# Row stores over all DMA engines, and k loaded in 1 KB pieces for the first two batches

## The chip, the core and the metric

The kernel runs on one core of one Trainium2 chip. The metric is the device time of one execution in microseconds; the runs of one kernel lie mostly within 0.3% of their median, so differences of 2 us out of 930 need several runs. The core has TensorE (PE, its weight loads as PEld), VectorE (DVE), ScalarE (ACT), GpSimd (POOL), and the sync engine (SP), which here issues almost all DMAs. All runs below were in the fast state.

## The reference

```python
kv  = np.einsum('bhsd,bhse->bhde', k, v)          # 8 batches, 8 heads, 576 rows, 64 wide
out = np.einsum('bhsd,bhde->bhse', q, kv)
rms = np.sqrt(np.mean(out * out, axis=-1, keepdims=True) + 1e-06)
x   = (out / rms * g_norm)                        # -> (4608, 512)
h   = x @ w_in                                    # 512 -> 2048
g   = np.maximum(h, 0.0) + np.log1p(np.exp(-np.abs(h)))
y   = g @ w_out                                   # 2048 -> 512
```

## The kernel before

All work is entered as tasks with an engine, a planned duration in ns and a priority (`pos`). At build time a small scheduler in the kernel orders the tasks of each engine; at run time each engine goes through its list in that order. 40 tuned numbers (`P0`) give priorities to the first weights (conversion and fetch), the first tiles and batches, and the later weights. While TensorE has nothing planned before the first matmul of the MLP (the two products with w_in and w_out), filler matmuls (`warm`) are put in, which are meant to keep its clock up.

The sums kv. Of each batch there are four loads of k and of v, each with the first 512 rows of two heads, four neighbouring rows to a partition (4 x 64 numbers, 1 KB), and one tail with the last 64 rows of all heads:

```python
x = new(s, [P, H, D])
src = src[b, p::NP, :MAIN].rearrange("h (s i) d -> s h i d", i=4)
if s is ks:
    for h in range(2):
        nc.sync.dma_start(out=x[:, h::2], in_=src[:, h])       # 256 B pieces
else:
    nc.sync.dma_start(out=x.rearrange("s (h i) d -> s h i d", h=2), in_=src)   # 1 KB pieces
# ... (cut)
for i in range(4):
    # l: two heads of k side by side, r: the same two heads of v
    nc.tensor.matmul(kv[:, i if tail else p], lhsT=l, rhs=r, ...)   # 128 x 128, half of it unused
last = add("PE", 820, run, lds + [last], pos + 0.5 * p, ...)
```

x leaves for DRAM in blocks of three tiles (TB = 3, 384 rows). From tile 12 on it is transposed in 32 x 32 blocks by VectorE and written three tiles together, which permutes the rows within a block; the result of a tile therefore leaves in up to four pieces of 32 rows:

```python
if ph == LAST and t >= BY_PE:
    n, i = divmod(t, TB)
    def store():
        m = 0
        while m < P // BL:                        # BL = 32
            a, u = divmod(P // BL * i + m, TB)
            k = min(TB - u, P // BL - m)
            nc.sync.dma_start(
                out=out[n * NT:(n + 1) * NT].rearrange("(t s) f -> t s f", t=TB)[u:u + k, a * BL:(a + 1) * BL],
                in_=ot.tile[m * BL:(m + k) * BL])
            m += k
    part[ph, t] = None, add("SP", 800, store, [a], pos, [], [ot], 750)
    return
dst = out[t * P:(t + 1) * P] if ph == LAST else ...            # whole rows of earlier tiles
```

The head of the program, which the experiments come to:

```python
for e in range(2):
    nc.scalar.dma_start(out=g_col[e * D:(e + 1) * D], in_=...)
nc.scalar.mul(g_down, g_col, DOWN_G)
nc.scalar.preload_act_table_set("softplus")
scratch = kv_diag[0][:, 0]
make_identity(nc, scratch)
```

## Time and profile before

| | before |
|---|---|
| time, median of 3 | 934.63 us |
| span of the profiled run | 932.7 us |
| TensorE idle, 0 to 55 us | 11.4 us |
| filler matmuls, 0 to 55 us | 43, 15.9 us |
| TensorE idle, 55 to 916.3 us | 0.04 us |
| from the last matmul to the end | 16.4 us |

TensorE's time can be read as three parts: a start in which it is idle, filled or busy by turns; a long middle in which it is always busy; and an end in which only data leave. The start and the end are what this change can move. The lines that carry this stand in the prediction.

### The profile page before, as it was taken

To read this page: it belongs to the slowest core of one execution; us is meant where nothing else is said; L and a number is where in the kernel's file an instruction comes from. 1 tells how busy PE (TensorE), PEld (TensorE's weight loads), DVE (VectorE), ACT (ScalarE), POOL (GpSimd) and SP (SyncE) were. 2 spreads that over 40 slices of the span, in tenths; PEclk is the share of its full clock that TensorE was granted. 3 is DMA by queue.
4 is the path that set the end of the run, shared out by engine and by line. 5 is a ranking of instruction groups with operands and counts; after the bars stand their busy time and mean duration, and the time that the engine had idled before them with its cause. 6 is when DMAs were issued, how large, how long until landed. Compare 5 with 4: busy or idle time off the path is not lost.

```text
span 932.7 us, 13257 instructions
## 1 busy us (share of the span) xinstructions
PE 904.9 (97%) x4821; PEld 818.5 (88%) x4821; DVE 627.3 (67%) x1055; ACT 414.5 (44%) x799; POOL 80.4 (9%) x78
## 2 busy tenths in 40 slices
PE   7899999999999999999999999999999999999992
PEld 5689899989999999999999999989999998999992
DVE  6777788776458887788757878887434455655531
ACT  4766555444433656464424455555322323333320
POOL 0323421221113100000000000000000000000000
PEclk8999999999999999999999999999999999999997
DMA  8999998498782554346334445551231233444321
GB/s 213 225 225 222 248 212 205 102 212 151 171 143 90 147 147 136 112 145 206 102 102 128 148 157 169 189 182 39 85 102 56 81 102 102 106 119 127 109 75 42
DMA packets 231377, 131.43 MB, mean 141 GB/s; under 512 B 130448, under 2 KB 205200, under 8 KB 231312
## 3 DMA queue, kind: packets, MB, share of 16 engines
q1 hardware_dynamic: 231152, 130.58, 53.3%
q8 instruction: 38, 0.62, 0.3%
q14 instruction: 27, 0.22, 0.1%
q10 hardware_dynamic: 160, 0.00, 0.0%
HBM read 91.75 MB, written 38.80 MB: 140 GB/s over the span
## 4 chain that ended last, share of the span: by engine, by line
PE 93%; SPq 2%; DVE 1%; DMA 1%; POOL 1%; ACT 1%; issue 0%; ACTq 0%
PE s L665 43%; PE h L658 43%; PE o L523 3%; PE o L506 3%; SPq L568 1%; DMA g_col<-in_g_norm_dram 1%; PE tp L540 0%; POOL r L532 0%; DMA m<-in_v_dram 0%; DMA qa<-in_q_dram 0%; DVE m L312 0%; PE tp L578 0%; DVE r L528 0%; DVE xv L440 0%; DVE m L316 0%
## 5 line engine op out<-in xcount | busy, mean ns | idle before, releaser
L658 PE MATMUL h<-xv,w 128*128 128x384 f32 x2304 | 434.6, 337 | 0.0
L665 PE MATMUL s<-w,gv 128*128 128x512 f32 x1728 | 434.3, 395 | 0.0
L658 PEld LDWEIGHTS h<-xv,w 128*128 128x128 f32 x2304 | 406.2, 188 | 14.8 <-issue 0.2
L665 PEld LDWEIGHTS s<-w,gv 128*128 128x128 f32 x1728 | 319.5, 188 | 59.1 <-issue 0.5
L678 ACT ACTIVATE g<-h 128x384 f32<-128x384 f32 x192 | 94.3, 491 | 398.4 <-PE h L658 394.4
L669 DVE TENSOR_TENSOR gv<-g,gv 128x384 fp32r<-128x384 f32 x192 | 106.6, 555 | 175.9 <-ACT gv L680 175.0
L680 ACT ACTIVATE gv<-g 128x384 fp32r<-128x384 f32 x192 | 100.9, 525 | 23.3 <-PE s L665 16.6
L673 DVE SCALAR_TENSOR_TENSOR gv<-gv 128x384 fp32r<-128x384 f32 x192 | 107.0, 557 | 6.0
L440 DVE SCALAR_TENSOR_TENSOR xv<-m,g_col,xv 128x512 fp32r<-128x512 f32 x102 | 75.8, 743 | 1.1 <-ACT xv L437 1.1
L444 DVE SCALAR_TENSOR_TENSOR xv<-xv 128x512 fp32r<-128x512 f32 x108 | 74.5, 690 | 2.6
L437 ACT ACTIVATE xv<-m,g_down 128x512 fp32r<-128x512 f32 x102 | 69.7, 710 | 2.5 <-DMA m<-x 2.4
L532 POOL TENSOR_TENSOR r<-r,half 128x8 f32<-128x8 f32 x36 | 65.8, 1826 | 3.0
L506 PEld LDWEIGHTS o<-m,m 128*128 128x128 f32 x256 | 34.2, 200 | 8.7 <-issue 7.3
L506 PE MATMUL o<-m,m 128*128 128x128 f32 x256 | 35.4, 285 | 6.4 <-DMA m<-in_v_dram 6.4
L705 DVE SCALAR_TENSOR_TENSOR m<-s,scale,m 128x512 f32<-128x512 f32 x24 | 17.9, 747 | 29.7 <-PE s L665 29.7
L523 PE MATMUL o<-kv_diag,m 128*128 128x128 f32 (+1 forms) x296 | 36.9, 275 | 0.0
L523 PEld LDWEIGHTS o<-kv_diag,m 128*128 128x128 f32 (+1 forms) x296 | 35.0, 179 | 1.8 <-issue 1.0
L531 POOL TENSOR_SCALAR r<-r 128x8 f32<-128x8 f32 x36 | 13.9, 386 | 244.9 <-DVE r L528 244.8
L535 DVE TENSOR_TENSOR x<-o,r 128x512 f32<-128x512 f32 x33 | 22.7, 688 | 17.6 <-POOL r L532 17.6
L528 DVE TENSOR_REDUCE r<-x 128x8 f32<-128x512 f32 x36 | 24.5, 681 | 13.3 <-ACT x L591 13.2
L705 DVE SCALAR_TENSOR_TENSOR m<-s,m 128x512 f32<-128x512 f32 x36 | 23.3, 684 | 10.2 <-PE s L665 10.1
L286 ACT ACTIVATE sq<-raw 128x512 bf16<-128x512 bf16 x32 | 21.3, 665 | 16.4 <-DMA raw<-in_moe_w_in_dram 10.2
(67 smaller groups left out, 445.6 us busy)
## 6 DMA issues: line engine op xcount, KB each, us to landing
m<-x SPq DMA_DIRECT2D x102, 256.0 KB
part<-m SPq DMA_DIRECT2D x72, 256.0 KB
m<-part SPq DMA_DIRECT2D x72, 256.0 KB
raw<-in_moe_w_in_dram SPq DMA_DIRECT2D x16, 512.0 KB
m<-in_k_dram SPq DMA_DIRECT2D x64, 128.0 KB
m<-in_v_dram SPq DMA_DIRECT2D x32, 256.0 KB
raw<-in_moe_w_out_dram SPq DMA_DIRECT2D x16, 512.0 KB
qa<-in_q_dram SPq DMA_DIRECT2D x24, 288.0 KB
```

What stands on the lines that cost most here:

```text
L437: nc.scalar.activation(cols(0, F32R), x.tile, func=AF.Identity, scale=g_down)
L440: nc.vector.scalar_tensor_tensor(out=cols(1, F32R), in0=x.tile, scalar=g_col, in1=cols(0), op0=ALU.mult, op1=ALU.subtract)
L444: nc.vector.scalar_tensor_tensor(out=cols(2, F32R), in0=cols(1), scalar=-RADIX, in1=cols(0), op0=ALU.mult, op1=ALU.add)
L506: nc.tensor.matmul(kv[:, i if tail else p], lhsT=l, rhs=r, start=(p == 0 and i == 0), stop=tail, skip_group_check=True)
L523: nc.tensor.matmul(y[r0:r0 + n, p::NP], lhsT=qT.tile[:, p, r0:r0 + n], rhs=kv_diag[b % 2][:, p].rearrange("r (h d) -> r h d", d=D), start= ...
L532: nc.gpsimd.tensor_tensor(out=r.tile, in0=r.tile, in1=half, op=ALU.pow)
L658: nc.tensor.matmul(hp, lhsT=w_in.tile[:, i, kd * P:(kd + 1) * P], rhs=xv.tile[:, i, kd], start=(m == 0), stop=(m == 3 * KD - 1))
L665: nc.tensor.matmul(mine[i].tile, lhsT=gv.tile[:, m, i * P:(i + 1) * P], rhs=w_out.tile[:, m], start=(c == cs[0] and m == 0), stop=(c == cs ...
L669: nc.vector.tensor_tensor(out=gv.tile[:, 1], in0=g.tile, in1=gv.tile.bitcast(F32)[:, 0], op=ALU.subtract)
L673: nc.vector.scalar_tensor_tensor(out=gv.tile[:, 2], in0=f32[:, 1], scalar=-RADIX, in1=f32[:, 0], op0=ALU.mult, op1=ALU.add)
L678: a = add("ACT", 490, lambda: nc.scalar.activation(new(g, [P, NT]), h.tile, func=AF.Softplus, scale=1.0 + E), [a], s, [g], [h])
L680: a = add("ACT", 530, lambda: nc.scalar.activation(new(gv, [P, 3, NT], F32R)[:, 0], g.tile, func=AF.Copy, scale=DOWN), [a], s, [gv])
```

## The change

The intent is to let the last results leave over all DMA engines, and to get the first k sooner. In the diff the 40 priorities are cut to their first three.

```diff
-    P0 = [-93.0, -6.2, -50.8, ...]      # 40 numbers
+    P0 = [-71.0, -4.7, -70.3, ...]
@@ kv_of
+        wide_rows = b < 2
-                if s is ks:
+                if s is ks and not wide_rows:
@@ run
+                    if wide_rows and not tail:
+                        for e in range(2):
+                            l, r = (x.tile.rearrange("s (h i) d -> s h i d", h=2)[:, e, i] for x in (ks, vs))
+                            nc.tensor.matmul(kv[e * D:(e + 1) * D, p, e], lhsT=l, rhs=r, ...)   # 64 x 64
+                        continue
-            last = add("PE", 820, run, ...
+            last = add("PE", 1640 if wide_rows and not tail else 820, run, ...
@@ rows: x of the last block is written tile by tile
+        g = TB if n < n_blocks - 1 else 1
+        i0, i = i - i % g, i % g
@@ leave
-        if ph == LAST and t >= BY_PE:
+        if ph == LAST and BY_PE <= t < n_tiles - TB:
-                (the while loop over k tiles)
+                for m in range(P // BL):
+                    a, u = divmod(P // BL * i + m, TB)
+                    row = n * NT + u * P + a * BL
+                    nc.sync.dma_start(out=out[row:row + BL], in_=ot.tile[m * BL:(m + 1) * BL])
```

The sums go a head at a time with this layout: the four rows of a head now lie side by side, so the same row of two heads no longer does. Not printed above are the planned durations that follow: 500 ns for a wide k load instead of 900, and 1600 ns for the four stores of a tile instead of 800.

More of the change, by code (lines that the diff above doesn't have):

```diff
@@ L184 @@
     LAST = PHASES[-1]
-    P0 = [-93.0, -6.2, -50.8, -8.7, -11.6, -1.5, -14.9, 2.7, -53.5, -34.8, -51.7, -14.7, -24.2, 1.3,
-          -0.2, -4.2, 2.5, -13.0, 8.5, 9.5, 5.5, 23.5, -2.0, 2.5, 2.5, 7.0, 5.0, 14.5, 9.0, 44.5, 49.5,
-          68.5, 52.5, 72.0, 95.5, 100.5, 114.5, 111.0, 116.5, 8.5]
+    P0 = [-71.0, -4.7, -70.3, -8.7, -15.1, -0.5, -23.9, 2.7, -65.0, -28.3, -35.2, -10.7, -25.2, 1.3,
+          -0.2, -2.7, 0.5, -17.5, 13.0, 9.5, 5.5, 6.5, -2.0, 2.5, 2.5, 28.0, 15.0, 14.5, 8.5, 44.5,
+          49.5, 68.5, 52.5, 72.0, 94.5, 99.5, 115.5, 110.5, 114.5, 8.5]
     CONVERT, FETCH, EARLY, LATER = P0[:8], P0[8:16], P0[16:27], P0[27:]
@@ L495, in kv_of @@
                        620 if tail else size, behind=int(pos - 2) - 3)
-                   for src, s, ns, size in ((k, ks, 900, 1300), (v, vs, 500, 850))]
+                   for src, s, ns, size in ((k, ks, *((500, 850) if wide_rows and not tail else (900, 1300))), (v, vs, 500, 850))]
             def run(ks=ks, vs=vs, p=p, tail=tail, n=n):
@@ L500, in run @@
                 for i in range(4):
+                    if wide_rows and not tail:
+                        for e in range(2):
+                            l, r = (x.tile.rearrange("s (h i) d -> s h i d", h=2)[:, e, i] for x in (ks, vs))
+                            nc.tensor.matmul(kv[e * D:(e + 1) * D, p, e], lhsT=l, rhs=r, start=(p == 0 and i == 0),
+                                             stop=False, skip_group_check=True)
+                        continue
                     if tail:
@@ L507, in run @@
                                      skip_group_check=True)
-            last = add("PE", 820, run, lds + [last], pos + 0.5 * p,
+            last = add("PE", 1640 if wide_rows and not tail else 820, run, lds + [last], pos + 0.5 * p,
                        [bank] if p == 0 else [], [ks, vs])
@@ L613, in turn_blocks @@
             if i == 0:
-                new(xb, [P, d_model // BL, TB, BL])
+                new(xb, [P, d_model // BL, g, BL])
             nc.vector.transpose(out=xb.tile[:, :, i], in_=x.tile.rearrange("p h d -> p (h d)").rearrange(
@@ L618, in store @@
         def store(a):
-            nc.sync.dma_start(out=xd[n][:, a * TB * BL:(a + 1) * TB * BL].rearrange("(b i) m -> i b m", i=BL),
+            nc.sync.dma_start(out=xd[n][:, i0 * P + a * g * BL:i0 * P + (a + 1) * g * BL].rearrange("(b i) m -> i b m", i=BL),
                               in_=xb.tile[a * BL:(a + 1) * BL].rearrange("i b t j -> i b (t j)"))
         turns.append(add("DVE", 710, turn_blocks, [a], pos, [] if i else [xb], [x], follows=turns[-1] if i else None))
-        if i == TB - 1:
-            stores = [add("SP", 450, lambda a=a: store(a), turns, pos + 0.5, [], [xb], 820) for a in range(P // BL)]
-            for u in range(n * TB, t + 1):
+        if i == g - 1:
+            stores = [add("SP", 450, lambda a=a: store(a), turns, pos + 0.5, [], [xb], 820 if g > 1 else 490)
+                      for a in range(P // BL)]
+            for u in range(t - i, t + 1):
                 x_there[u] = stores
@@ L707, in leave @@
                 op0=ALU.mult, op1=ALU.add), [done, ld] + (scale_done if ph == LAST else []), pos, [ot], [bank, pt])
-        if ph == LAST and t >= BY_PE:
+        if ph == LAST and BY_PE <= t < n_tiles - TB:
             n, i = divmod(t, TB)
             def store():
-                m = 0
-                while m < P // BL:
+                for m in range(P // BL):
                     a, u = divmod(P // BL * i + m, TB)
-                    k = min(TB - u, P // BL - m)
-                    nc.sync.dma_start(
-                        out=out[n * NT:(n + 1) * NT].rearrange("(t s) f -> t s f", t=TB)[u:u + k, a * BL:(a + 1) * BL],
-                        in_=ot.tile[m * BL:(m + k) * BL])
-                    m += k
-            part[ph, t] = None, add("SP", 800, store, [a], pos, [], [ot], 750)
+                    row = n * NT + u * P + a * BL
+                    nc.sync.dma_start(out=out[row:row + BL], in_=ot.tile[m * BL:(m + 1) * BL])
+            part[ph, t] = None, add("SP", 1600, store, [a], pos, [], [ot], 750)
             return
```

## The prediction

> **What bounds the kernel now.** I read the views in this order: the page's busy shares, then one table of busy time by stage, then the two ends of the run in finer stretches with the sync engine's waits, then the groups of TensorE instructions by shape. First the stage table, cut where TensorE changes behaviour (columns: busy microseconds and instruction count of each engine, granted TensorE clock, DMA share, GB/s).
>
> ```profile
> 0.00:22.50 22.50, 16.01 (x66) 11.87 (x67) 13.95 (x28) 10.91 (x19) 0.69 (x6) 0.85 0.83 215
> 22.50:55.00 32.50, 27.58 (x188) 22.95 (x187) 25.78 (x43) 23.24 (x48) 10.94 (x10) 1.00 0.88 214
> 55.00:916.30 861.30, 861.26 (x4572) 783.63 (x4571) 586.86 (x985) 380.32 (x733) 68.73 (x63) 1.00 0.52 138
> 916.30:932.70 16.40, 0.00 (x0) 0.00 (x0) 0.75 (x2) 0.00 (x0) 0.00 (x0) 0.59 0.21 48
> ```
>
> From 55.0 to 916.3 us TensorE is busy 861.26 of 861.30 us at full clock. Nothing in the change removes TensorE work there, so that stretch can't shrink. What can is at the ends: 16.4 us after the last matmul, and a start where TensorE idles 6.5 us of the first 22.5 and 4.9 us of the next 32.5. The start holds a hidden reserve too: the filler matmuls that only keep the clock up (line 778) count as busy.
>
> ```profile
> 22.50:55.00 32.50, 7.48 (x22) 3.57 (x22) 1.00 0.88 214
> ```
>
> That is the second stage of the table for line 778 alone, TensorE busy first. Idle plus filler in 22.5 to 55 us is 4.9 + 7.5 = 12.4 us; before 22.5 us it is 6.5 + 8.45 = 15 us, mostly spent waiting for the first k and v, some of it unavoidable.
>
> The end. The first fence is the timeline, the second the sync engine's waits, the third short stretches (same columns as the stage table).
>
> ```profile
> 916.30 0.75 DVE L705 SCALAR_TENSOR_TENSOR m<-s,scale,m 128x512 f32<-128x512 f32 x1
> ...
> 915.69 1.21 SPq L716 DMA_DIRECT2D out_dram<-m  x2
> 917.01 1.53 SPq L716 DMA_DIRECT2D out_dram<-x  x2
> 918.64 1.29 SPq L716 DMA_DIRECT2D out_dram<-m  x2
> ```
>
> ```profile
> SPq L809 <- DMA out_dram<-m: 11.6, 1, 11.6
> ```
>
> ```profile
> 921.00:925.00 4.00, 0.00 (x0) 0.00 (x0) 0.00 (x0) 0.00 (x0) 0.00 (x0) 0.50 0.23 58
> ...
> 931.00:931.50 0.50, 0.00 (x0) 0.00 (x0) 0.00 (x0) 0.00 (x0) 0.00 (x0) 0.50 0.03 12
> 931.50:932.00 0.50, 0.00 (x0) 0.00 (x0) 0.00 (x0) 0.00 (x0) 0.00 (x0) 0.50 0.00 0
> ```
>
> The last add ends at 917.05, the last store is issued by 919.9, and the program then waits 11.6 us for it at some 50 to 60 GB/s. Bytes stop by 931.5 and the span ends 1.2 us later. The same 256 KB of results stored as whole rows, at 750.29 us (line 724, 0.35 us to issue), look quite different:
>
> ```profile
> 750.00:751.00 1.00, 1.00 (x6) 0.87 (x5) 0.96 (x3) 0.47 (x1) 0.00 (x0) 1.00 0.00 0
> 751.00:752.00 1.00, 1.00 (x8) 1.00 (x7) 1.00 (x3) 0.00 (x0) 0.00 (x0) 1.00 0.70 262
> 752.00:752.50 0.50, 0.50 (x5) 0.50 (x4) 0.50 (x1) 0.00 (x0) 0.00 (x0) 1.00 0.00 0
> ```
>
> All 262 KB move inside 751 to 752: done 1.7 us after the issue began.
>
> **What the Trainium skill says.** "DMA: Bandwidth & Descriptors", section "Why a DMA increments its semaphore by 16 and not by 1": a DMA is split over the largest number of engines, at most 16, that divides the slowest non-unit dimension of both sides; and the lowest-numbered ones are taken. The old store has an outer dimension of 1 to 3 (tiles) on the DRAM side, so it should use 2 or 3 engines. The trace agrees: 48 to 58 GB/s in the drain against 262 for the whole-row store. Check by bytes: in the last block the three tiles put 64 KB (three engines), 128 KB (two) and 64 KB (three) on engine 0, plus 8 KB from the two 64 KB pieces, 264 KB. At 262/16 = 16.4 GB/s an engine needs 16 us; about 917 to 931.2 was measured (14.2 us, 18.6 GB/s), the right size.
>
> Same page, "Specifications": transfers need pieces of at least 512 B for line rate. The old k loads scatter 256 B pieces, v uses 1 KB. The trace agrees in kind: 374 GB/s at 4.4 to 5.0 us, a v-rich stretch, but 266 at 8 to 11 us, where 1747 of 2107 packets are under 512 B.
>
> "TensorE: Matmul & The Clock Gate", "LDWEIGHTS (loading the stationary operand)": the time goes with the columns of the stationary operand. The trace agrees, for these fp32 loads:
>
> ```profile
> L506 PEld LDWEIGHTS o<-m,m 128*128 128x128 f32 x256 | 34.2, 200 | 8.7 <-issue 7.3
> L523 PEld LDWEIGHTS o<-kv_diag,m 128*128 128x128 f32 x232 | 29.6, 191 | 0.8
> ...
> L523 PEld LDWEIGHTS o<-kv_diag,m 128*64 128x64 f32 x64 | 5.4, 136 | 1.0 <-issue 1.0
> ```
>
> **The change part by part.** (1) Stores of tiles 12 to 32: four DMAs of 32 rows (16 engines each, as 32 divides by 16) instead of two over 1 to 3 engines or 16. More issues on the sync queue, some 4 x 0.4 against 2 x 0.65 us, in a stage where the queue waits most of the time for results (line 716 waited 13.7 us for one) and TensorE is full: worth 0.
>
> (2) The last block of x is written one tile at a time, so its results are whole contiguous tiles, each one 256 KB store. Cost: 12 writes of 128 B pieces in place of 4 of 384 B, 6144 packets against 2048, in the first third, where DMA isn't what TensorE waits for: 0. Gain, at the end: the adds end at 915.66, 916.36 and 917.05. The last store is issued at about 917.07, its bytes have moved by 917.07 + 1.7 = 918.8, the receipt by some 919, and with the old 1.2 us from the last bytes to the end the span closes near 920.2. Against 932.7 this is 12.5 us; I take 12.4.
>
> (3) k of batches 0 and 1, eight loads of 256 KB, in 1 KB pieces and one DMA instead of two. Engine time: 0.262 MB at 266 GB/s is 0.99 us, at 374 GB/s 0.70, so 0.29 us a load, 1.15 us a batch. Sync queue: two issues took 1.2 to 1.35 us, one like v's 0.62, so 0.6 us a load; between 13 and 62 us that queue issues with hardly a gap. Another 2 us: the queue sits from 9.1 to 12.67 us on a weight load that waits 3.5 us for its buffer, ahead of the fourth k and v of batch 0, and no byte moves from 12.5 to 13.5. With the shorter durations the kernel's own scheduler can put the fourth k and v before it. Batch 0 should be summed some 3 us sooner, and in batch 1 another 1.15 us is saved: 4.2 us of data time.
>
> (4) The summation for these batches: 8 matmuls 64 x 64 instead of 4 of 128 x 128 per step, each as two instructions in the trace. Now 8 instructions take about 0.89 us, 111 ns each. The 64-column form of line 523 ran 16 in some 1.35 us, 84 ns each, so with 64 moving columns too I estimate 57 to 65 ns: 16 x 60 = 0.96 us, about the same. Were it 111 ns regardless of size, 0.89 x 8 steps = 7 us, put where filler and idle stood: little of it reaches the path.
>
> (5) New priorities: the first three tiles closer together and ahead of some weight conversions, batch 1 earlier, reloads of x and partial sums much earlier. In the first chain the tiles went through normalisation at 31.3, 35.7 and 40.4 us, 4.4 us apart, though the slow GpSimd step takes some 2.5 us, so there is room. But VectorE is already 25.8 of 32.5 us busy, and the change removes none of its work. I add nothing for it and take nothing off.
>
> Sum: 934.6 - 12.4 - 4.2 = 918.0; a little less of the start's gain should arrive, so 918.2.
>
> **The rivals.** A: the start gains nothing, as VectorE and the conversions set it (for: 79% busy in 22.5 to 55 us, and GpSimd's round trip in the chain; against: TensorE waited 6.4 us in all for v). Then only the tail remains: 922.2. B: the start gains much more, since tuned priorities bring the first MLP matmul, at 46.4 us, forward and turn the 12.4 us of filler and idle into work: 8 us or so, 914. C: the drain isn't cured, since the store's landing is slow in itself: 930; against it stand the 1.7 us at 750 us. D: earlier reloads hold buffers or block the in-order sync queue and open gaps in the full stretch, a few us lost; nothing shows it in the old trace, where that stretch has 0.04 us idle.
>
> **Range and chances.** The tail is well determined, 11.5 to 13. The start is the uncertain term, about 0 to 8 us. That gives 913.5 to 922.5. For faster by over 2% the time must fall below 915.9, a start gain over 6.3 us: rival B, 0.25. Slower by 2% needs D in a severe form: 0.01. The rest, 0.74, lies within 2%.
>
> **What would show it.** Right: three last stores of one DMA each, the final wait for the output 1.5 to 2.5 us instead of 11.6, TensorE's last matmul at about 912, and the end about 4 us after it. Fourth k and v issued before the 3.5 us wait, batch 0's last sum at about 18.5 instead of 21.5 us, the 64-wide sums at 57 to 65 ns an instruction, TensorE full by about 51 us. Wrong: a drain still under 100 GB/s; TensorE's end at 916 (start gain lost) or under 909 (priorities worth more than the data); gaps between 55 and 900 us.

## The result, and the profile after

| | before | after |
|---|---|---|
| time, median of 6 | 934.66 us | 918.38 us |
| range | 932.99 to 936.76 | 917.23 to 920.66 |
| ratio of the fast runs | | 0.9829, 95% interval 0.9811 to 0.9846 |
| span of the profiled run | 932.7 us | 917.5 us |
| from the start of the last add to the end | 16.4 us | 3.9 us |
| start of the last add | 916.30 us | 913.63 us |
| filler matmuls | 43 | 21 |

A ratio is the mean time of one kernel's fast runs over that of the other's in the same rounds, so it isn't quite the quotient of the medians.

The end of the changed kernel, on the timeline of the sync queue and of VectorE (start, duration, what):

```profile
913.63 0.75 DVE L715 SCALAR_TENSOR_TENSOR m<-s,scale,m 128x512 f32<-128x512 f32 x1
...
913.01 0.35 SPq L730 DMA_DIRECT2D out_dram<-m  x1
913.72 0.35 SPq L730 DMA_DIRECT2D out_dram<-x  x1
914.40 0.33 SPq L730 DMA_DIRECT2D out_dram<-m  x1
```

Its wait at the end, in the list of the sync queue's waits (total, times, longest):

```profile
SPq L815 <- DMA out_dram<-m: 1.7, 1, 1.7
```

And its last stretches, with the columns of the stage table:

```profile
914.00:915.00 1.00, 0.00 (x0) 0.00 (x0) 0.38 (x1) 0.00 (x0) 0.00 (x0) 1.00 1.00 371
915.00:916.00 1.00, 0.00 (x0) 0.00 (x0) 0.00 (x0) 0.00 (x0) 0.00 (x0) 1.00 0.98 367
```

Beside them, a stretch of the old drain:

```profile
925.00:929.00 4.00, 0.00 (x0) 0.00 (x0) 0.00 (x0) 0.00 (x0) 0.00 (x0) 0.50 0.13 48
```

The DMA share (the last number but one) is the mean busy share of the core's 16 engines. In the old drain it is 0.13, two engines of sixteen; in the new one 1.00, all of them. Two is also what the prediction's count of bytes leaves at that time: engines 0 and 1 get 264 KB, the third only 136 (64 + 64 + 8), so it is done first. A busy engine moves about 23 GB/s in both (48 over two, 371 over sixteen). So the trace itself shows that the number of engines made the drain slow.

Three issues of a third of a microsecond, 370 GB/s in place of 50 to 60, and a wait of 1.7 in place of 11.6 us. The end is 12.5 us shorter. The rest, 916.30 - 913.63 = 2.7 us in this pair of profiles, comes from the start; the middle is full in both. The start's gain differs from run to run: a second profile of the changed kernel ended at 915.5 us.

The stage table of the changed kernel, the same first two stretches as before:

```profile
0.00:22.50 22.50, 13.29 (x92) 9.68 (x93) 13.24 (x27) 10.88 (x19) 0.69 (x6) 1.00 0.79 226
22.50:55.00 32.50, 26.25 (x224) 21.68 (x224) 25.38 (x42) 23.21 (x48) 11.18 (x10) 1.00 0.92 242
```

TensorE is busy less, not more: 39.5 us of the first 55 instead of 43.6. A busy share doesn't show progress here, as 9.0 us of filler stand in it instead of 15.9. What counts is idle time, filler, and whether the kernel's own work takes longer. The stage table and the filler's line give, from 0 to the start of the last add, these microseconds of TensorE ("other" is what is left, so the three sum to the last column; the ends of matmuls are modelled in the profile, so a few tenths mean nothing):

| profile | idle | filler | other | last add starts |
|---|---|---|---|---|
| before | 11.45 | 15.93 | 888.92 | 916.30 |
| changed | 15.50 | 8.99 | 889.14 | 913.63 |
| changed again (a2_after) | 14.16 | 9.00 | 888.49 | 911.65 |
| k only (e2_k) | 14.98 | 9.71 | 892.71 | 917.40 |
| priorities only (e3_prio) | 10.40 | 15.42 | 888.57 | 914.39 |
| k and priorities (e6_prio_k) | 14.22 | 8.90 | 889.59 | 912.71 |

The change takes away 6.9 us of filler and adds 4.1 us of idle time. The start of the first MLP matmul, which the texts below use as a mark, is a weaker one: it came at 42.66 instead of 46.38 us, but 3.7 us sooner there became 2.7 at the end; the second profile has it at 42.56 and ends 2 us sooner than the first; and with the priorities alone it came at 46.65, later than before, and yet the last add started 1.9 us sooner.

### The profile page after: what moved, and what is told of

Read it like the earlier page. It is cut to its first block, busy times and chain, and to the rows that moved or that the text cites. A ratio compares the mean times of both kernels' runs of the same rounds, so it can differ in the third digit from the quotient of the medians.

```text
span 917.5 us, 13377 instructions
## 1 busy us (share of the span) xinstructions
PE 898.1 (98%) x4863; PEld 812.4 (89%) x4863; DVE 626.6 (68%) x1055; ACT 415.1 (45%) x799; POOL 81.2 (9%) x78
## 4 chain that ended last, share of the span: by engine, by line
PE 95%; DMA 2%; DVE 1%; ACT 1%; SPq 0%; issue 0%; ACTq 0%
PE s L675 44%; PE h L668 43%; PE o L530 3%; PE o L513 3%; DMA m<-in_v_dram 1%; DMA g_col<-in_g_norm_dram 1%; PE tp L547 0%; DMA tail<-in_k_dram 0%; SPq L608 0%; PE o L505 0%; PE h L367 0%; DVE xv L440 0%; DVE xv L444 0%; PE tp L585 0%; ACT L750 0%
## 5 line engine op out<-in xcount | busy, mean ns | idle before, releaser
L668 PEld LDWEIGHTS h<-xv,w 128*128 128x128 f32 x2304 | 406.6, 188 | 15.9 <-ACT g L688 1.1
L538 POOL TENSOR_SCALAR r<-r 128x8 f32<-128x8 f32 x36 | 15.1, 419 | 240.9 <-DVE r L535 240.6
L715 DVE SCALAR_TENSOR_TENSOR m<-s,m 128x512 f32<-128x512 f32 x36 | 23.7, 684 | 13.5 <-PE s L675 13.4
L542 DVE TENSOR_TENSOR x<-o,r 128x512 f32<-128x512 f32 x33 | 22.7, 687 | 13.5 <-POOL r L539 13.4
L303 ACT ACTIVATE sq<-sq,big 128x512 bf16<-128x512 bf16 x32 | 22.9, 717 | 11.2 <-DVE m L299 11.1
L286 ACT ACTIVATE sq<-raw 128x512 bf16<-128x512 bf16 x32 | 21.2, 664 | 12.5 <-DMA raw<-in_moe_w_in_dram 8.3
L299 DVE SCALAR_TENSOR_TENSOR m<-sq,m 128x512 f32<-128x512 bf16 x32 | 22.1, 690 | 6.3 <-ACT sq L286 4.9
```

Of the source, the lines that this page charges most:

```text
L668: nc.tensor.matmul(hp, lhsT=w_in.tile[:, i, kd * P:(kd + 1) * P], rhs=xv.tile[:, i, kd], start=(m == 0), stop=(m == 3 * KD - 1))
L715: a = add("DVE", 700, lambda: nc.vector.scalar_tensor_tensor(out=new(ot, [P, d_model]), in0=bank.tile, scalar=(scale if ph == LAST else 1. ...
```

## The experiments

Twelve runs, of eleven kernels, went in three jobs, each with 5 rounds beside the kernel before. All gave correct results. Microseconds below are the ratio less 1, times the job's median of before (934.0, 934.9 and 934.5 us).

| kernel | ratio | 95% interval | against before |
|---|---|---|---|
| end only | 0.9870 | 0.9857 to 0.9883 | -12.1 us |
| row stores only | 0.9909 | 0.9896 to 0.9923 | -8.5 |
| k only | 1.0024 | 1.0016 to 1.0031 | +2.2 |
| priorities only | 0.9979 | 0.9973 to 0.9986 | -2.0 |
| k and priorities | 0.9959 | 0.9947 to 0.9971 | -3.8 |
| end and priorities | 0.9857 | 0.9842 to 0.9871 | -13.4 |
| k and weights' priorities | 0.9973 | 0.9961 to 0.9984 | -2.5 |
| k and tiles' priorities | 0.9985 | 0.9978 to 0.9992 | -1.4 |
| changed kernel again | 0.9831 | 0.9817 to 0.9846 | -15.8 |
| changed, sums planned shorter | 0.9838 | 0.9825 to 0.9852 | -15.1 |
| changed, ScalarE freed | 0.9805 | 0.9792 to 0.9819 | -18.2 |
| the same again | 0.9794 | 0.9781 to 0.9807 | -19.2 |

The theory was the prediction's: the end and the start are separate gains, and the start's comes from k's data. The main rival for the start was that the new priorities make it.

### The end alone

```diff
+ last block of x by tile, row stores; P0, k loads and sums as before
```

> The kernel before with only the new stores and the last block of x by tile; old k loads, old priorities. Theory (the end and the start are separate gains): the drain goes as in the changed kernel, the start stays, so 12.5 us less than before, about 922.2 us, ratio 0.9866; the last matmul stays near 916.3 us and the span ends 3.9 us after it. Rival (the drain is short in the changed kernel only because its schedule differs): clearly less than 10 us gained.

922.14 us, ratio 0.9870. The rival falls: the end's gain doesn't need the rest of the change. The span (920.7 us) ends 3.9 us after the start of the last add, as in the changed kernel.

### Row stores alone

```diff
-                while m < P // BL: ...            (k tiles in one DMA)
+                for m in range(P // BL): ...      (four DMAs of 32 rows)
  last block of x still written three tiles together
```

> The kernel before with only the row stores over 16 engines (four DMAs a tile from tile 12 on); the last block of x still written three tiles together, so its results too leave in four pieces a tile. Theory (the drain was the few engines): most of the drain goes; twelve issues of about 0.45 us from 915.7 us on end near 921, then 1.7 us for the last bytes and 1.2 us to the end: about 924 us of span, 926 of time, ratio 0.991. Rival (the row stores are worth nothing at the end, and the last block by tile makes all of the gain): ratio 1.000, a wait of over 10 us for the output at the end.

926.34 us, ratio 0.9909, as expected: some 8.5 of the 12 us. The timeline of its sync queue shows what is left:

```profile
918.60 1.78 SPq L715 DMA_DIRECT2D out_dram<-x  x4
920.48 1.79 SPq L715 DMA_DIRECT2D out_dram<-m  x4
```

Its last wait for the output is 1.3 us, so the engines are no longer the limit; the queue needs 1.8 us to issue four DMAs, and the last tile's issue ends at 922.3 us, 4.2 us after its result was ready (its add ended at 918.1 us). So two costs of the end are apart now: few engines a DMA (cured by 32 rows outermost), and the issues of the row stores, twelve for the last block instead of three (cured by writing it in whole tiles).

### k alone, priorities alone, and both

```diff
  e2: k loads and sums of the change;  P0 and stores as before
  e3: P0 of the change;                k and stores as before
  e6: both;                            stores as before
  e4: P0 and stores of the change;     k as before
```

> The kernel before with only the k loads in 1 KB pieces and the sums by head for batches 0 and 1; old stores, old priorities. Theory of the prediction (the data of k sets the start): the whole start gain of the changed kernel, 2.7 us as read from the end of its last matmul (916.26 to 913.59 us), so about 932 us, ratio 0.997; the drain of 11.6 us stays. Rival (the new priorities make the start's gain): 0, ratio 1.000. Second rival (only both together, as the priorities were tuned for the new loads): 0 or a loss.

> The kernel before with only the 40 new priority numbers. Theory of the prediction: 0, ratio 1.000. Rival (priorities make the start's gain): 2.7 us less, ratio 0.997. Second rival (they fit the new loads only): a loss of 1 us or more, last matmul after 917 us.

> The kernel before with the new k loads and sums and the new priorities, old stores. The k part alone was 2.2 us slower, the priorities alone 1.9 us faster. If the parts add up: 934.3 us, ratio 1.000. If the priorities were fitted to the new loads (they only pay together): below the priorities alone, about 930.3 to 931 us, ratio 0.996, last matmul near 913.6 us as in the changed kernel.

> The changed kernel with the old k loads and sums put back: new stores, last block by tile, new priorities. Theory of the prediction: as the stores alone, 922.2 us, ratio 0.9866, last matmul near 916.3 us. Rival (priorities make the start's gain): as the changed kernel, 918.4 us, ratio 0.983. Second rival: slower than the stores alone, above 923 us.

k alone is slower by 2.2 us, priorities alone are faster by 2.0, and both together are faster by 3.8. Added up, the parts would give a loss of 0.2 us; so they work together, and no single theory of the three holds as it stood. With the end cured the same shows: 0.9857 without k, 0.9829 and 0.9831 with it (in other jobs, and with intervals that overlap a little).

The data did come sooner with k alone. The first 40 us of before, then of k alone:

```profile
0.00:40.00 40.00, 30.83 (x165) 23.95 (x165) 29.05 (x53) 25.12 (x47) 8.03 (x12) 0.91 0.86 217
```

```profile
0.00:40.00 40.00, 27.92 (x217) 21.20 (x217) 28.69 (x52) 23.12 (x43) 6.05 (x12) 0.79 0.88 243
```

243 against 217 GB/s over 40 us is 1 MB more. The last sum of batch 1, its tail, shows it on TensorE; before, then k alone:

```profile
42.46 1.05 PE L506 MATMUL o<-tail,tail 128*128 128x128 f32 x8
```

```profile
38.50 1.61 PE L513 MATMUL o<-tail,tail 128*128 128x128 f32 x8
```

That is 4.0 us sooner. But from 55 to 100 us, where before is full, TensorE has gaps; first before, then k alone, then k with the new weights' priorities:

```profile
55.00:100.00 45.00, 45.00 (x306) 41.93 (x306) 33.05 (x56) 27.31 (x54) 14.99 (x15) 1.00 1.06 235
```

```profile
55.00:100.00 45.00, 42.93 (x283) 38.51 (x282) 32.24 (x54) 27.70 (x55) 14.81 (x14) 1.00 1.03 212
```

```profile
55.00:100.00 45.00, 45.00 (x302) 42.05 (x301) 36.05 (x61) 29.30 (x57) 17.40 (x16) 1.00 1.04 221
```

What TensorE waited for in k alone after 55 us:

```profile
PE h L665 <- ACT w L370: 1.4, 1, 1.4
PE o L513 <- DMA m<-in_v_dram: 0.6, 1, 0.6
```

Line 370 makes the third part of a weight. So the data came sooner, the order of the rest stayed as it had been tuned for the old loads, and TensorE stood idle for 2.07 us, for a weight that wasn't converted in time and a v that came late. These gaps aren't the whole loss. By the table of idle and filler, k alone has 3.5 us more idle time than before (2.07 of it after 55 us) and 6.2 less filler, but the other work took 3.8 us longer. Part of that is seen in the trace: from 36 to 40 us the granted clock was 0.56 to 0.59, and 16 sums at 36.16 us took 1.08 us instead of 0.69. With the priorities added (k and priorities) it took 3.1 us less again, and idle time and filler 1.6 us less together. Why the order does this isn't settled. "k alone" also holds three things, the loads, the sums by head and their planned durations, which weren't run apart.

### Which priorities

```diff
  e10: k of the change + first 16 of the new P0 (conversion and fetch of the first weights)
  e11: k of the change + new P0[16:27] (first tiles, batches, reloads)
```

> The new k loads and sums with only the first 16 new priority numbers (order of the first weights' loads and conversions); old stores, the other 24 numbers old. The k part alone lost 2.2 us, in its trace partly in waits of TensorE for converted weights after 55 us. Theory A (the order of the weights is what the new loads needed): about 931 us, ratio 0.996, no wait of TensorE for a weight after 55 us. Theory B (the order of the first tiles and batches is what they needed): 936 us, ratio 1.002, as the k part alone.

> The new k loads and sums with only the 11 new numbers for the first tiles, batches and reloads; old stores, weights in the old order. Theory A (weights' order): 936 us, ratio 1.002. Theory B (tiles' order): about 931 us, ratio 0.996. If both are needed: both kernels of this pair stay above 933 us.

Either half turns the loss into a gain: 932.4 us with the weights' order, 932.85 with the tiles'. With the weights' order theory A's mark is there (no gap after 55 us), but theory B isn't refuted: with the tiles' order 1.4 us of gaps remain (TensorE is busy 43.59 of 45 us), and that kernel still gains 1.4 us on before. Neither half has the 930.62 us of all the priorities together (another job, and for the weights' half the intervals overlap). The last 13 of the 40 numbers, for the later weights, weren't run apart. How the shares arise one by one isn't settled.

### The scheduler's number for a sum

```diff
-  last = add("PE", 1640 if wide_rows and not tail else 820, run, ...
+  last = add("PE", 620 if wide_rows and not tail else 820, run, ...
```

> The changed kernel with one number of its own scheduler changed: a sum by head is planned at 620 ns of TensorE, about what a warm one takes in the trace, instead of 1640. Theory (the too long plan leaves TensorE without filler, so its clock falls and the sums of the start run at half rate): more filler matmuls than 21, no cold sums after 14 us, and 0.5 to 2 us less, 916.5 to 918. Rival (the cold stretch costs nothing on the path, and any other number unsettles priorities tuned to 1640): the same or slower, 918.4 to 921.

919.69 us, ratio 0.9838: no gain, as the rival said; the interval overlaps those of the changed kernel, so a loss isn't shown either. There were more filler matmuls, 35, but the trace of this kernel on TensorE shows what they did:

```profile
19.31 1.12 PE L505 MATMUL o<-m,m 128*64 128x64 f32 x16
20.36 2.87 PE L784 MATMUL h<-ident_r 128*128 128x512 f32 x6
23.07 1.05 PE L513 MATMUL o<-tail,tail 128*128 128x128 f32 x8
```

The sums here are still cold, that is, at a lower clock than later: 16 instructions take 1.12 us, against 0.69 later in the changed kernel. And six filler matmuls stand for 2.7 us between them and batch 0's tail, which starts at 23.07 us instead of 19.67. Its data were there: its last load was issued at 15.58 us, and the trace gives 3.4 us from issue to landing. In an in-order queue, filler planned for time that isn't there delays real work. By the measure of the table above, filler rose by 6.3 us, idle time fell by 4.1 and the other work by 1.7, and the last add started 0.6 us later, at 914.18.

The expectation had said that no sum would be cold after 14 us. They stayed cold, so this run shows that the planned number isn't worth correcting by itself; what warm sums would be worth it doesn't show.

### ScalarE freed at the start

What the predicted start gain stumbled over is on the timeline of the changed kernel, ScalarE first, then the sync queue:

```profile
7.75 1.28 ACT L749 ACT_TABLE_LOAD   x1 [7.75 <-DMA g_col<-in_g_norm_dram]
9.05 0.20 ACT L749 ACTIVATE g_down<-g_col 128x1 f32<-128x1 f32 x1
9.27 1.28 ACT L750 ACT_TABLE_LOAD   x1
10.56 0.31 ACT L754 ACTIVATE minus_r<-ident_r 128x128 fp32r<-128x128 f32 x1
10.78 0.65 ACT L286 ACTIVATE sq<-raw 128x512 bf16<-128x512 bf16 x1
```

```profile
8.11 0.47 SPq L493 DMA_DIRECT2D m<-in_v_dram  x1
13.42 0.34 SPq L275 DMA_DIRECT2D raw<-in_moe_w_out_dram  x1
13.80 1.39 SPq L483 DMA_DIRECT2D tail<-in_k_dram  x2
```

ScalarE's first instruction needs g, whose DMA was issued at 0.72 us and holds it until 7.75; two table loads stand before its first weight; only at 10.78 us does it begin the first weight, whose data VectorE had already begun to use at 5.45. That weight holds its buffer, so the queue sits from 8.6 to 13.42 us, now with all four k and v pairs issued but not the tails.

```diff
-    nc.scalar.mul(g_down, g_col, DOWN_G)
     nc.scalar.preload_act_table_set("softplus")
     scratch = kv_diag[0][:, 0]
     make_identity(nc, scratch)
+    nc.gpsimd.tensor_scalar(out=g_down, in0=g_col, scalar1=DOWN_G, scalar2=None, op0=ALU.mult)
```

> The changed kernel, with ScalarE freed of its first wait: the scaled g is computed on GpSimd, and the softplus table is loaded first, so ScalarE no longer sits until 7.75 us for g and then loads two tables until 10.6 us. Theory (late ScalarE holds the first weight buffer, so the sync queue sits from 8.6 to 13.4 us and no byte moves for some 1.5 us: this ate the missing part of the predicted start gain): the first weight's square starts at about 5.5 instead of 10.8 us, the queue's wait shrinks to under 2 us, the first MLP matmul comes 2 us or more sooner than 42.7 us, and the time falls by 1.5 to 4 us, to 915 to 917. Rival (VectorE's conversion work sets the start, whatever the queue does): within 1 us of the changed kernel.

916.5 us, ratio 0.9805. On the timeline of this kernel:

```profile
5.36 0.67 ACT L286 ACTIVATE sq<-raw 128x512 bf16<-128x512 bf16 x1 [1.82 <-DMA raw<-in_moe_w_in_dram]
```

```profile
8.64 0.47 SPq L493 DMA_DIRECT2D m<-in_v_dram  x1
9.24 0.38 SPq L275 DMA_DIRECT2D raw<-in_moe_w_out_dram  x1
```

The longest wait of a weight load in the queue (line 275) fell from 4.8 to 1.3 us, and the next weight's load went out 4.2 us sooner. The first MLP matmul came at 42.00 us, only 0.7 us sooner, less than expected; but the last add started at 910.81 instead of 913.63 us, with 11.94 us of idle time before it instead of 15.50. To be sure of the gain both kernels ran again side by side:

> The changed kernel again, unchanged, to stand beside the freed ScalarE on the same chip and in the same rounds: about 918.5 us, ratio 0.983; in its profile the cold TensorE stretch up to about 22 us, as in the other runs with the new sums.

> The changed kernel with ScalarE freed, again: if its gain is real, 1.5 to 3 us below the changed kernel of the same rounds, ratio 0.980 to 0.981; if it was the chip or the rounds, the same ratio as the changed kernel.

918.54 and 915.56 us; 0.9831 (0.9817 to 0.9846) and 0.9794 (0.9781 to 0.9807). The intervals don't meet: freeing ScalarE is worth some 3 us more, and this version beats both kernels. In this pair the first MLP matmul started at 42.56 and 40.86 us. These two profiles don't show the gain, though: their last adds start at 911.65 and 911.31 us, as the profiled run of the changed kernel was the fastest of its five and that of the freed one the slowest of its four. The edit removes the wait for g and one of the two table loads at once, so their shares aren't apart.

## Why the prediction was right, point by point

The time (918.2 predicted, 918.38 measured) and the sizes of both terms of the sum held. The mechanism of the end held too. For the start the reason given was wrong in part, so that its size came out right is partly luck.

1. The end: 12.4 us predicted, 12.1 measured with the end alone, and 12.5 in the traces. The last store's bytes in 1.7 us from issue (914.40 to 916.1), the wait of 1.5 to 2.5 us (1.7): right. From the last bytes to the end it is 1.4 us, not 1.2: in finer slices the old kernel's bytes had stopped by 931.25, not 931.5. TensorE's last matmul, said to end at about 912, ended at 913.6 (911.6 in the second profile). Rival C falls.
2. Row stores "worth 0" for tiles 12 to 32: right for the full middle. On the last block, where the step didn't look, they alone would have brought 8.5 us.
3. The start: 4.2 us predicted. k and priorities together brought 3.8 us against before (interval 2.7 to 5.0); the end alone against the whole, -12.1 and -15.8, leaves 3.7. The size is right, but the step "I add nothing for it and take nothing off" on the priorities failed: without them the k loads lose 2.2 us, and they gain 2.0 us alone. The step that counted 4.2 us of data time as TensorE's gain mistook data that are there for work that is in order: with k alone batch 1's tail did start 4.0 us sooner, and the kernel was 2.2 us slower.
4. Batch 0's tail: "some 3 us sooner" was 1.9 us (21.53 to 19.67). The fourth k and v did go out before the queue's wait, at 7.70 and 8.11 us. But the wait itself grew from 3.5 to 4.8 us, and in TensorE's order the third and fourth sums stood behind a matmul on the first weight, for which it waited 2.7 us. I had seen the wait and put it down to the schedule; with ScalarE freed the wait before the tails was gone (the queue goes on at 9.24 us, 0.1 us after the fourth v), and the tail starts at 18.10 us, 3.4 us sooner than before.
5. The sums: 57 to 65 ns an instruction was predicted. Warm they take 38 ns: on the changed kernel's timeline 16 of them start at 27.04, and the next work at 27.65 us.

```profile
27.04 0.69 PE L505 MATMUL o<-m,m 128*64 128x64 f32 x16
27.65 1.16 PE L530 MATMUL s<-kv_diag,m 128*128 128x128 f32 x8
```

   So a step takes 0.61 us instead of 0.89; the estimate erred on the safe side. Batch 0's sums, which were cold, took 60 ns (32 of them from 17.17 to 19.08 us): inside the range, but for another reason than the one it was worked out from. The scheduler's 1640 ns is 2.7 times a warm step, and correcting it alone didn't pay.
6. Rival D: no idle time of TensorE between 55 and 910 us in the changed kernel. TensorE was full from 53.3 us, a little later than the 51 named. One reading was off without effect: the GpSimd step, put at 2.5 us, takes 1.7 to 2.1 us in the first 60 us of the trace.

## What to carry to other kernels

Look at what leaves last: if the final wait moves bytes at a fraction of the rate seen elsewhere in the same trace, count the outermost dimension of that store before anything else, and then the issues. In a kernel with fixed orders, faster data are worth what the order can use; test a load and the priorities that go with it together, each alone, and neither. Measure such a start by idle time, filler and the length of the other work together, not by when one matmul begins. And when an in-order queue waits for a buffer, follow the holder of the buffer back to its engine's first instruction.

## What the Trainium skill lacked or had wrong

- "DMA: Bandwidth & Descriptors", "Specifications", gives about 27 GiB/s (29 GB/s) an engine. Here a busy engine moved about 23 GB/s, with two busy (48 GB/s) as with all sixteen (371 GB/s). The rule for the number of engines, in "Why a DMA increments its semaphore by 16 and not by 1", agreed with the trace.
- "TensorE: Matmul & The Clock Gate", "Back-to-back issue gap", gives about 60 cycles for 1 to 64 columns and 134 for 128; that section has no row for fp32. Here an fp32 matmul appears as two instructions, each of 111 ns for 128 x 128 and 38 ns for 64 x 64.
- The same page, "Seeing it yourself", warns that the clock's trace events can be unreliable. This case agrees: the changed kernel's profile shows a clock of 1.00 up to 22.5 us, another profile of the same kernel 0.77, and in both the same 32 sums at 17 us take 1.9 us, 60 ns each, against 38 ns warm. The duration of a known matmul was the better thermometer.
- No page that I used says that filler matmuls in an in-order queue can delay what stands behind them: six held up one tail for 2.7 us here.
